# Transposing half of the activations by DMA instead of TensorE, with the contraction re-cut into chunks of 128 rows

## The chip, the cores and the metric

One core of a Trainium2 chip. The metric is the device time of one execution in microseconds (us), lower is better; medians of several executions are given. Times of the same kernel differ a little from chip to chip, so a kernel is compared only with runs of the kernel before on the same chip.

Names used below: PE is TensorE's matmul stream, PEld its weight loads, DVE is VectorE, ACT is ScalarE, POOL is GpSimd, SP is SyncE, which here only issues DMAs.

## The reference

The input `x` has 2048 tokens of 448 features. Two branches start from it and are mixed by a gate for each token.

```python
g = sigmoid((x * gate_w).sum(-1, keepdims=True))
a = A_ref(x, wq, wk, wv, wo, beta)      # q,k,v = x @ wq, x @ wk, x @ wv; 16 heads of 28; 4 segments of 512
                                        # causal softmax inside a segment + linear memory of earlier segments
b = B_ref(x, w1, b1, w2, b2)            # h = layernorm(x); u = gelu(h^T w1 + b1); y = u w2 + b2 (MLP over tokens)
return g * a + (1 - g) * b              # ... all else cut
```

For this change, two things matter. The projections `x @ wk` and so on need `x` with features on the partitions, that is, transposed. The MLP over tokens needs `x` as it is, but normalized.

## The kernel before

The kernel is a list of operations (`op`), each with an engine, an estimated cost, a priority and the buffers that it reads and writes. A planner walks through an estimated clock and gives each free engine its ready operation of best priority. What comes out is one fixed order of instructions for each engine. The chip runs that order: in the traces, the matmuls behind a waiting matmul wait with it (in e7 below, no matmul starts for 0.63 us while one waits). The kernel lets TensorE write its results to banks of PSUM, and uses a bank again when another engine has copied it out (an eviction).

```python
CK = 112                                   # contraction rows of a chunk; 4 * 112 = 448
...
load_x("SP", 0, 2)                         # tokens 0..255
op("SP", ... dma_start(wk_nat[0:CK], WK.rearrange("(c p) d -> p c d", p=CK)) ...)
load_x("SP", 2, 2)
op("ACT", ... dma_start(wvx[0:CK, :, D : D + 1], GW.rearrange("(c p o) -> p c o", p=CK, o=1) ...)   # gate_w
op("SP", ... wq, then wv, then x of tokens 512.. in blocks of 512 ...)
...
def transposes(tc):                        # token chunk tc: 512 tokens
    for half in range(2):
        ...                                # 8 PE transposes into one PSUM bank
                last = e.matmul(tb[0:CK, at : at + 128], xh[:, 4 * tc + ti, c * CK : c * CK + CK], ident[:, :],
                                is_transpose=True, start=True, stop=True, skip_group_check=True)
        ...                                # then the eviction to xT, by DVE or ACT as the planner likes
            op("DVE", lambda e, io=io: e.tensor_copy(*io()), **buse(b), reads=[bres(b)], writes=[R_xT[tc][half]],
               name=f"xTcp{tc}_{half}", cost=dve_cost(1024, 2), prio=P_PROJ + tc - 150,
               alt=("ACT", lambda e, io=io: e.activation(*io(), ACT.Copy), act_cost(1024)))

def proj_d(w_pad, R_w, hg, tc, b, t0=0, n=512):   # a projection: four matmuls over the four chunks
        for c in range(NCT):
            last = e.matmul(bank(b)[:, 0:n], w_pad[0:CK, c, hg * 128 : hg * 128 + 128],
                            xT[0:CK, c, tc * 512 + t0 : tc * 512 + t0 + n], start=(c == 0), stop=(c == NCT - 1), ...)
...
PRJ = (P_PROJ, P_PROJ + 1, P_M1 + 8.5, P_M2 + 4.5)   # chunk 2 is projected only after the MLP's unit 8
...
transposes(0); ...
for tc in (1, 2, 3):
    transposes(tc)
for t in range(NT):
    ln_stats(t)                            # DVE: statistics of the layer norm, 16 tiles
ln_coef()                                  # POOL: 1/sqrt(var), a power of 2.9 us
for t in range(NT):
    ln_apply(t)                            # DVE; the MLP's matmuls read the result
```

The order in time is: load, chunk 0 transposed and projected, chunks 1 to 3 transposed, layer norm, and then attention, MLP and the remaining projections woven together.

## Time and profile before

| | before |
|---|---|
| median time (3 runs) | 189.0 us (188.65 to 189.43) |
| span of the profiled execution | 186.4 us |
| PE busy in the span | 180.6 us, 97% |
| first projection starts | 7.80 us |
| last matmul starts | 183.64 us |
| PE transposes | 64, of which 32 for chunks 2 and 3 |

The head of the page of the kernel before gives the span and the busy time of each engine, with its share of the span and its number of instructions:

```profile
span 186.4 us, 3493 instructions
PE 180.6 (97%) x1373; PEld 87.3 (47%) x1384; DVE 154.0 (83%) x319; ACT 133.5 (72%) x171; POOL 69.6 (37%) x93
```

PE is the engine to shorten. A listed matmul time is a latency, though. Matmuls overlap, and what one costs PE is the distance from its start to the next start. The view of PE in time order of the kernel before has the columns start, length from the first start to the last end, line and operation, number of matmuls, and the idle time ahead of them:

```profile
15.45 1.50 PE L558 MATMUL t<-t 128*112 128x128 bf16 x24
...
30.57 0.29 PE L783 MATMUL t<-t 28*128 28x256 bf16 x4 [0.32 <-ACT t L792]
30.79 1.71 PE L646 MATMUL t<-t 112*128 112x449 bf16 x8
32.34 1.02 PE L589 MATMUL t<-t 112*128 112x512 bf16 x4
...
33.63 0.73 PE L820 MATMUL t<-t 128*32 128x512 bf16 x16
34.29 1.83 PE L889 MATMUL t<-t 128*128 128x448 bf16 x8
```

Line 558 is the PE transpose: 24 of them take 1.35 us from first start to what follows (the chain of waits gives that figure), 56 ns each. Line 889 is the MLP: its first matmul starts at 34.29 us. Projections of chunk 1 (lines 646 and 589) fill PE until the layer norm is ready, almost without a gap.

The waits of PE in the kernel before (line that waited, what it waited for, total us, times, longest us) confirm how few gaps there are:

```profile
PE t L528 <- DVE t L486: 1.2, 1, 1.2
PE t L589 <- ACT t L574: 0.4, 1, 0.4
PE t L783 <- ACT t L792: 0.3, 1, 0.3
```

The first is the warm-up ahead of all work. The others are 0.7 us in all (two lines of 0.3 us are left out).

At the head of the kernel PE waits for data. The chain of waits of the kernel before, cut to its first 8 us (start, us, what):

```profile
1.31 4.82 DMA t<-in_A_wk_dram
...
6.16 0.63 DVE t L536
6.79 0.34 DVE t L571
...
7.15 0.61 ACT t L574
...
7.80 0.28 PE t L589
```

The load of wk lands at 6.13 us. Then come the padding of wk (L536), two evictions (L571, L574) and the first projection (L589). The busy time of each engine in stretches of 2 us of the kernel before (the stretch and its length, then busy us and number of instructions of each engine, the clock granted to PE, the share of the DMA engines, GB/s):

```profile
core 0: us, PE busy (x) PEld busy (x) DVE busy (x) ACT busy (x) POOL busy (x), PEclk, DMA share, GB/s
...
2.00:4.00 2.00, 2.00 (x6) 0.76 (x5) 0.00 (x0) 0.54 (x1) 2.00 (x2) 1.00 0.48 111
4.00:6.00 2.00, 2.00 (x13) 1.06 (x12) 1.18 (x3) 0.00 (x0) 1.86 (x4) 1.00 1.05 340
```

From 2 to 4 us only 111 GB/s arrive, and from 4 to 6 us 340.

The layer norm's coefficients run on POOL. In time order, POOL in the kernel before:

```profile
26.93 0.21 POOL L741 TENSOR_SCALAR t<-t 128x16 f32<-128x16 f32 x1 [21.07 <-DVE t L734]
27.22 2.92 POOL L742 TENSOR_TENSOR t<-t 128x16 f32<-128x16 f32 x1
```

They can't start before DVE has the last statistics, at 26.9 us.

### The profile page before, as it was taken

How to read it: one execution, taken by the hardware profiler on the slowest of the kernel's cores; microseconds unless marked ns; L12 is line 12 of the kernel's file. 1: busy time of each engine (PE TensorE's matmuls, PEld its weight loads, DVE VectorE, ACT ScalarE, POOL GpSimd, SP SyncE). 2: the span in 40 equal slices, each digit the busy share in tenths (PEclk: the TensorE clock that was granted, in tenths of full speed). 3: DMA queues.
4: the chain of work that ended last, by engine and by line, in shares of the span. 5: the costliest groups of instructions: out<-in, count | busy, mean ns of one | idle time of the engine just before them, and what ended most of it. 6: DMA issues, size and time to landing. Idle time of an engine off the chain costs nothing.

```text
span 186.4 us, 3493 instructions
## 1 busy us (share of the span) xinstructions
PE 180.6 (97%) x1373; PEld 87.3 (47%) x1384; DVE 154.0 (83%) x319; ACT 133.5 (72%) x171; POOL 69.6 (37%) x93
## 2 busy tenths in 40 slices
PE   7999999999999999999999999999999999999994
PEld 2658434344454444434454443454454444454554
DVE  1979898998689989798998999998999987765232
ACT  2288779968999999999988979840399857620230
POOL 8200029343242534543725635171135365160200
PEclk9999999999999999999999999999999999999999
DMA  3999991001971746001341506238810072744011
GB/s 92 321 328 265 294 150 28 5 0 40 250 220 31 204 116 159 4 4 28 96 133 37 160 4 183 45 102 225 240 35 0 4 213 70 212 146 127 0 53 49
DMA packets 42596, 21.77 MB, mean 117 GB/s; under 512 B 8148, under 2 KB 42580, under 8 KB 42580
## 3 DMA queue, kind: packets, MB, share of 16 engines
q1 hardware_dynamic: 42116, 21.54, 43.7%
q8 instruction: 11, 0.18, 0.4%
q10 hardware_dynamic: 464, 0.00, 0.1%
q14 instruction: 5, 0.04, 0.1%
HBM read 18.13 MB, written 1.84 MB: 107 GB/s over the span
## 4 chain that ended last, share of the span: by engine, by line
PE 82%; DVE 6%; ACT 6%; DMA 3%; issue 1%; SPq 0%
PE t L889 24%; PE t L917 24%; PE t L589 9%; PE t L783 7%; PE t L869 6%; PE t L820 6%; PE t L646 3%; ACT t L792 3%; DMA t<-in_A_wk_dram 3%; DVE t L732 2%; PE t L670 1%; ACT t L631 1%; PE t L558 1%; DVE t L581 1%; DVE t L624 1%
## 5 line engine op out<-in xcount | busy, mean ns | idle before, releaser
L792 ACT ACTIVATE t<-t 128x2048 bf16<-128x2048 f32 (+1 forms) x48 | 76.9, 1601 | 12.5 <-PE t L783 12.2
L796 POOL TENSOR_SCALAR_AFFINE_SELECT t<-t 128x512 bf16<-128x512 bf16 x64 | 47.0, 737 | 64.2 <-ACT t L792 59.9
L889 PE MATMUL t<-t 128*128 128x448 bf16 x224 | 47.3, 353 | 0.4 <-issue 0.3
L917 PE MATMUL t<-t 128*128 128x448 bf16 (+1 forms) x238 | 46.0, 342 | 0.3
L917 PEld LDWEIGHTS t<-t 128*128 128x128 bf16 x238 | 22.2, 98 | 19.4 <-issue 1.7
L589 PE MATMUL t<-t 112*128 112x512 bf16 (+1 forms) x144 | 30.0, 356 | 0.4 <-ACT t L574 0.4
L889 PEld LDWEIGHTS t<-t 128*128 128x128 bf16 x224 | 20.2, 98 | 20.4 <-issue 2.6
L849 POOL TENSOR_TENSOR t<-t 128x448 bf16<-128x448 f32 x12 | 14.3, 1196 | 18.2 <-DVE t L847 18.2
L589 PEld LDWEIGHTS t<-t 112*128 112x128 bf16 x144 | 13.4, 98 | 13.1 <-issue 0.9
L922 DVE SCALAR_TENSOR_TENSOR t<-t 128x448 bf16<-128x448 f32 (+1 forms) x17 | 11.1, 653 | 10.0 <-PE t L917 7.5
L783 PE MATMUL t<-t 28*128 28x512 bf16 (+3 forms) x256 | 17.3, 302 | 0.8 <-ACT t L792 0.3
L875 ACT ACTIVATE t<-t 128x448 bf16<-128x448 f32 x9 | 6.6, 730 | 12.4 <-PE t L869 12.2
L646 PE MATMUL t<-t 112*128 112x449 bf16 x64 | 14.1, 354 | 0.1
L869 PE MATMUL t<-t 128*128 128x448 bf16 x64 | 13.6, 353 | 0.0
L835 DVE STREAM_TRANSPOSE t<-t 128x512 f32<-128x512 f32 x16 | 11.3, 703 | 2.6 <-PE t L820 2.6
L626 ACT ACTIVATE t<-t 128x512 bf16<-128x512 f32 x8 | 4.8, 595 | 11.4 <-PE t L589 11.4
L783 PEld LDWEIGHTS t<-t 28*128 28x128 bf16 x256 | 5.1, 91 | 16.3 <-ACT t L792 10.8
L855 DVE STREAM_TRANSPOSE t<-t 128x512 bf16<-128x512 bf16 x16 | 11.2, 698 | 1.6 <-POOL t L849 1.6
L732 DVE BATCH_NORM_STATS2 t<-t 128x6 f32<-128x448 bf16 x16 | 9.4, 611 | 3.5 <-DMA t<-in_A_x_dram 3.3
L820 PE MATMUL t<-t 128*32 128x512 bf16 (+3 forms) x256 | 11.6, 302 | 0.0
L906 DVE SCALAR_TENSOR_TENSOR t<-t 128x448 bf16<-128x448 f32 x14 | 9.2, 658 | 2.9 <-ACT t L904 2.8
L901 DVE SCALAR_TENSOR_TENSOR t<-t 128x448 f32<-128x448 f32 x14 | 9.7, 697 | 1.7 <-ACT t L896 1.7
(83 smaller groups left out, 216.1 us busy)
## 6 DMA issues: line engine op xcount, KB each, us to landing
t<-in_B_w_dram SPq DMA_DIRECT2D x7, 1024.0 KB, 6.0
t<-in_B_w_dram SPq DMA_DIRECT2D x8, 896.0 KB, 5.2
out_dram<-t SPq DMA_DIRECT2D x15, 112.0 KB, 3.0
t<-in_A_x_dram SPq DMA_DIRECT2D x3, 448.0 KB, 7.7
t<-in_A_x_dram SPq DMA_DIRECT2D x2, 224.0 KB, 4.4
t<-in_A_wk_dram SPq DMA_DIRECT2D x1, 392.0 KB, 4.8
t<-in_A_wq_dram SPq DMA_DIRECT2D x1, 392.0 KB, 5.8
t<-in_A_wv_dram SPq DMA_DIRECT2D x1, 392.0 KB, 6.6
```

The costliest lines, as they stand in the source:

```text
L589: last = e.matmul(bank(b)[:, 0:n], w_pad[0:CK, c, hg * 128 : hg * 128 + 128], xT[0:CK, c, tc * 512 + t0 : tc * 512 + t0 + n], start=(c == ...
L646: last = e.matmul(bank(b)[:, 0 : D + 1], xT[0:CK, c, t * 128 : t * 128 + 128], wvx[0:CK, c, :], start=(c == 0), stop=(c == NCT - 1), skip_ ...
L732: op("DVE", lambda e: e.bn_stats(st6[:, t, :], xh[:, t, :]), reads=[R_x[t]], writes=[R_st6[t]], name=f"bns{t}", cost=512, prio=P_PROJ - 10)
L783: last = e.matmul(bank(hl)[:, c0 : c0 + w_], kT[r, hg, s * 512 + j * 128 : s * 512 + j * 128 + 128], qT[r, hg, s * 512 + 128 * j : s * 512 ...
L792: op("ACT", lambda e: e.activation(pv, ps[:, 0:4, 0:w], ACT.Exp, scale=SCALE), reads=R_bank[0:4], writes=[R_P[u % 2][f]], name=f"exp{n}", ...
L796: op("POOL", lambda e, d=d: e.affine_select(d, d, pattern=[[0, 4], [1, 128]], compare_op=ALU.is_ge, fill=0.0, base=0, channel_multiplier=- ...
L820: last = e.matmul(bank(cb)[32 * hl : 32 * hl + 32, 128 * j : 512], vaug[:, 4 * s + j, 32 * h : 32 * h + 32], pv[:, hl, c0 : c0 + w_], star ...
L835: dv(lambda e: e.transpose(t2[:, 0, :], bank(cb)[:, 0:512]), [bres(cb)], [R_tt[tb][0]], "ta", 630, use=(cb,))
L849: op("POOL", lambda e: e.tensor_tensor(o3, n3[0], n3[1], op=ALU.add), reads=R_tt[tb], writes=[R_ob[tb]], name=f"o{u}", cost=1280, port=Tru ...
L869: last = e.matmul(bank(b)[:, 0:D], oT[:, hg, T * 128 : T * 128 + 128], wo_sb[:, hg, :], start=(hg == 0), stop=(hg == NHG - 1), skip_group_ ...
L889: op("PE", lambda e, st=st: e.matmul(bank(b)[:, 0:D], w1c[:, st, f2 * 128 : f2 * 128 + 128], xh[:, st, :], start=(st == 0), stop=(st == NT ...
L917: op("PE", lambda e, ft=ft: e.matmul(bank(b)[:, 0 : c1 - c0], w2c[:, ft, t2_ * 128 : t2_ * 128 + 128], uT[:, ft, c0:c1], start=(ft == 0), ...
```

## The change

The intent: chunks 2 and 3 of `x` are needed in transposed form only from 74.8 us on. So 32 of the 64 PE transposes can be replaced by transposes that the DMA engines make straight from DRAM, and PE, DVE and ACT get their time back. The builder accepts a DMA transpose only if its columns are a multiple of 128. (A kernel that kept the 112-row chunks did not build. The Trainium skill, "DMA: Bandwidth & Descriptors", DMA Transpose (X-bar), Constraints, says that for DRAM inputs with fewer than 128 columns software can fall back to a rearranged access pattern; this builder refused instead.) So the contraction is cut into 128-row chunks that start at rows 0, 128, 256 and 320. The fourth repeats 64 rows of the third, and the weights of these 64 rows are set to zero. For this, each weight matrix is loaded in two parts, the second from ACT's queue, and so the tiny load of `gate_w` moves from first to last on ACT's queue.

```diff
-CK = 112
+CK = 128
+C0 = (0, 128, 256, 320)
...
+    def load_w(dst, src, r, name):
+        op("SP", lambda e: e.dma_start(dst[:, 0:3, 0:D], src[0:384].rearrange("(c p) d -> p c d", p=128)), ...)
+        op("ACT", lambda e: e.dma_start(dst[64:128, 3, 0:D], src[384:448]), ...)
+
+    def transpose_x(tc):
+        for k, (c, n) in enumerate(((0, 3), (3, 1))):
+            op("SP", lambda e, c=c, n=n: e.dma_start_transpose(
+                xT[:, c : c + n, tc * 512 : tc * 512 + 512], x2[tc * 512 : tc * 512 + 512, C0[c] : C0[c] + 128 * n]),
+               writes=[R_xT[tc][k]], name=f"dtx{tc}_{k}", dma=True, cost=1200 * n, nbytes=180000 * n)
...
     load_x("SP", 0, 2)
-    op("SP", lambda e: e.dma_start(wk_nat[0:CK], WK.rearrange("(c p) d -> p c d", p=CK)), ...)
+    load_w(wk_nat, WK, R_P[0], "wk")
     load_x("SP", 2, 2)
-    op("ACT", lambda e: e.dma_start(wvx[0:CK, :, D : D + 1], GW.rearrange("(c p o) -> p c o", p=CK, o=1), ...
+    load_w(wq_nat, WQ, R_P[1], "wq")
+    load_w(wvx, WV, R_wv, "wv")
+    op("ACT", lambda e: e.dma_start(wvx[:, 0:3, D : D + 1], GW[0:384].rearrange("(c p o) -> p c o", p=128, o=1), ...
+    op("ACT", ... wvx[64:128, 3, D : D + 1], GW[384:448] ...)
+    for w, r, name in ((wk_nat, R_wz[0], "k"), (wq_nat, R_wz[1], "q"), (wvx, R_wz[2], "v")):
+        op("DVE", lambda e, w=w: e.memset(w[0:64, 3, :], 0.0), writes=[r], name="wz" + name, cost=200, prio=50.0)
...
-    for tc in (1, 2, 3):
-        transposes(tc)
+    transposes_1()                    # chunks 0 and 1 stay on PE, in 128-row form
...
     for _ in range(3):
         ring_load()                   # the first three blocks of w1
+    transpose_x(2)
+    transpose_x(3)
```

More of the change, by code (lines that the diff above doesn't have):

```diff
@@ L358, in build_kernel @@
     wqk = sb([128, 2, NCT, 512])
-    wvx = sb([128, NCT, D + 1])
+    wvx = sb([128, NCT, D + 4])
     wo_sb = sb([128, NHG, D])
@@ L409, in build_kernel @@
     R_wkp, R_wqp = R("wkp"), R("wqp")
-    R_wv, R_gw, R_wo = R("wv"), R("gw"), R("wo", 4)
+    R_wv, R_gw, R_wo, R_wz = R("wv", 2), R("gw", 2), R("wo", 4), R("wz", 3)
     R_qT = [R(f"qT{g}_", 4) for g in range(NHG)]
@@ L436, in load_x @@
            writes=R_x[t0 : t0 + n], name=f"ldx{t0}", dma=True, cost=500 if n == 2 else 1300, nbytes=n * 128 * 896)
+    def load_w(dst, src, r, name):
+        op("SP", lambda e: e.dma_start(dst[:, 0:3, 0:D], src[0:384].rearrange("(c p) d -> p c d", p=128)),
+           writes=[r[0]], name="ld" + name, dma=True, cost=500, nbytes=344064)
+        op("ACT", lambda e: e.dma_start(dst[64:128, 3, 0:D], src[384:448]), writes=[r[1]], name="ld" + name + "b",
+           dma=True, cost=500, nbytes=57344)
@@ L438, in build_kernel @@
+    def transpose_x(tc):
[3 more added lines that the diff above has]
+               writes=[R_xT[tc][k]], name=f"dtx{tc}_{k}", dma=True, cost=1200 * n, nbytes=180000 * n)
     load_x("SP", 0, 2)
-    op("SP", lambda e: e.dma_start(wk_nat[0:CK], WK.rearrange("(c p) d -> p c d", p=CK)), writes=R_P[0],
-       name="ldwk", dma=True, cost=500, nbytes=401408)
+    load_w(wk_nat, WK, R_P[0], "wk")
@@ L441, in build_kernel @@
     load_x("SP", 2, 2)
-    op("ACT", lambda e: e.dma_start(wvx[0:CK, :, D : D + 1], GW.rearrange("(c p o) -> p c o", p=CK, o=1),
+    load_w(wq_nat, WQ, R_P[1], "wq")
+    load_w(wvx, WV, R_wv, "wv")
+    op("ACT", lambda e: e.dma_start(wvx[:, 0:3, D : D + 1],
+                                     GW[0:384].rearrange("(c p o) -> p c o", p=128, o=1),
                                      allow_slow_non_contiguous=True),
-       writes=[R_gw], name="ldgw", dma=True, cost=500, nbytes=8000)
-    op("SP", lambda e: e.dma_start(wq_nat[0:CK], WQ.rearrange("(c p) d -> p c d", p=CK)), writes=R_P[1],
-       name="ldwq", dma=True, cost=500, nbytes=401408)
@@ L447, in build_kernel @@
-    op("SP", lambda e: e.dma_start(wvx[0:CK, :, 0:D], WV.rearrange("(c p) d -> p c d", p=CK)), writes=[R_wv],
-       name="ldwv", dma=True, cost=500, nbytes=401408)
-    for t0 in (4, 8, 12):
-        load_x("SP", t0, 4)
+       writes=[R_gw[0]], name="ldgw", dma=True, cost=500, nbytes=8000)
+    op("ACT", lambda e: e.dma_start(wvx[64:128, 3, D : D + 1], GW[384:448].rearrange("(p o) -> p o", o=1),
+                                     allow_slow_non_contiguous=True),
+       writes=[R_gw[1]], name="ldgwb", dma=True, cost=500, nbytes=2000)
@@ L451, in build_kernel @@
+    for w, r, name in ((wk_nat, R_wz[0], "k"), (wq_nat, R_wz[1], "q"), (wvx, R_wz[2], "v")):
+        op("DVE", lambda e, w=w: e.memset(w[0:64, 3, :], 0.0), writes=[r], name="wz" + name, cost=200, prio=50.0)
+    load_x("SP", 4, 4)
+    load_x("SP", 8, 4)
+    load_x("SP", 12, 4)
     op("SP", lambda e: e.dma_start(betab[:, :], BETA.partition_broadcast(128)), writes=[R_beta],
@@ L470, in ring_load @@
                                            w1v[:, :, k * 256 : k * 256 + 256]),
-               reads=[R_wv, R_gw], writes=[R_slot[r]], name=f"ldw1_{k}", dma=True, cost=500,
+               reads=R_wv, writes=[R_slot[r]], name=f"ldw1_{k}", dma=True, cost=500,
                nbytes=1048576)
@@ L511, in load_wo @@
                                                   WO.rearrange("(g l d) m -> l d g m", g=NHG, l=4)[hl]),
-               reads=[R_wv], writes=[R_wo[hl]], name=f"ldwo{hl}", dma=True, cost=500, nbytes=100352)
+               reads=[R_wv[0]], writes=[R_wo[hl]], name=f"ldwo{hl}", dma=True, cost=500, nbytes=100352)
     rr = [0]
@@ L537, in build_kernel @@
                                       wk_nat.rearrange("p c (h j) -> p (c h) j", j=DH)[0:CK]),
-       reads=R_P[0], writes=[R_wkp], name="padk", cost=560, port=True, prio=P_BASE)
+       reads=R_P[0] + [R_wz[0]], writes=[R_wkp], name="padk", cost=560, port=True, prio=P_BASE)
     def pad_q():
@@ L542, in pad_q, with transposes_0, fn, io @@
                                           wq_nat.rearrange("p c (h j) -> p (c h) j", j=DH)[0:CK]),
-           reads=R_P[1], writes=[R_wqp], name="padq", cost=560, port=True, prio=P_BASE)
-    def transposes(tc):
+           reads=R_P[1] + [R_wz[1]], writes=[R_wqp], name="padq", cost=560, port=True, prio=P_BASE)
+    def transposes_0(half):
+        b = next_bank()
+        def fn(e):
+            tb = bank(b).bitcast(BF16)
+            last = None
+            for c in range(4):
+                for k in range(2):
+                    last = e.matmul(tb[:, c * 256 + k * 128 : c * 256 + k * 128 + 128],
+                                    xh[:, 2 * half + k, C0[c] : C0[c] + 128], ident[:, :], is_transpose=True,
+                                    start=True, stop=True, skip_group_check=True)
+            return last
+        op("PE", fn, reads=R_x[2 * half : 2 * half + 2] + [R_ident], writes=[bres(b)], **btake(b), name=f"trx0_{half}",
+           mode="f", cost=8 * 56, prio=P_PROJ + 0.02 * half)
+        for k in range(2):
+            def io(k=k):
+                return (xT[:, 2 * k : 2 * k + 2, half * 256 : half * 256 + 256],
+                        bank(b).bitcast(BF16)[:, k * 512 : k * 512 + 512].rearrange("p (c t) -> p c t", c=2))
+            if k == 0 or half == 1:
+                op("DVE", lambda e, io=io: e.tensor_copy(*io()), reads=[bres(b)], writes=[R_xT0[half][k]],
+                   name=f"xTcp0_{half}{k}", cost=dve_cost(512, 2), prio=P_PROJ - 150)
+            else:
+                op("ACT", lambda e, io=io: e.activation(*io(), ACT.Copy), reads=[bres(b)], writes=[R_xT0[half][k]],
+                   name=f"xTcp0_{half}{k}", cost=act_cost(512), prio=P_PROJ - 150)
@@ L547, in transposes, with transposes_1, fn @@
+    def transposes_1():
         for half in range(2):
             b = next_bank()
-            parts = [(ti, c) for ti in range(4) for c in (2 * half, 2 * half + 1)]
-            if tc == 0:
-                parts = [(ti, c) for c in range(4) for ti in (2 * half, 2 * half + 1)]
-            def fn(e, b=b, parts=parts):
+            def fn(e, half=half, b=b):
                 tb = bank(b).bitcast(BF16)
                 last = None
-                for ti, c in parts:
-                    at = (c * 256 + ti % 2 * 128) if tc == 0 else (c % 2 * 512 + ti * 128)
-                    last = e.matmul(tb[0:CK, at : at + 128], xh[:, 4 * tc + ti, c * CK : c * CK + CK], ident[:, :],
-                                    is_transpose=True, start=True, stop=True, skip_group_check=True)
-                return last
@@ L562, in transposes @@
-            op("PE", fn, reads=[R_x[4 * tc + ti] for ti, c in parts] + [R_ident], writes=[bres(b)], **btake(b),
-               name=f"trx{tc}_{half}", mode="f", cost=8 * 56, prio=P_PROJ + (0.02 if tc == 0 and half else 0))
-            if tc == 0:
-                for k, on_dve in ((0, True), (1, half == 1)):
-                    def io(b=b, half=half, k=k):
-                        return (xT[0:CK, 2 * k : 2 * k + 2, half * 256 : half * 256 + 256],
-                                bank(b).bitcast(BF16)[0:CK, k * 512 : k * 512 + 512].rearrange("p (c t) -> p c t", c=2))
-                    if on_dve:
-                        op("DVE", lambda e, io=io: e.tensor_copy(*io()), reads=[bres(b)], writes=[R_xT0[half][k]],
-                           name=f"xTcp0_{half}{k}", cost=dve_cost(512, 2), prio=P_PROJ - 150)
-                    else:
-                        op("ACT", lambda e, io=io: e.activation(*io(), ACT.Copy), reads=[bres(b)],
-                           writes=[R_xT0[half][k]], name=f"xTcp0_{half}{k}", cost=act_cost(512), prio=P_PROJ - 150)
-            else:
-                def io(half=half, b=b):
-                    return (xT[0:CK, 2 * half : 2 * half + 2, tc * 512 : tc * 512 + 512],
-                            bank(b).bitcast(BF16)[0:CK, :].rearrange("p (c t) -> p c t", c=2))
-                op("DVE", lambda e, io=io: e.tensor_copy(*io()), **buse(b), reads=[bres(b)], writes=[R_xT[tc][half]],
-                   name=f"xTcp{tc}_{half}", cost=dve_cost(1024, 2), prio=P_PROJ + tc - 150,
-                   alt=("ACT", lambda e, io=io: e.activation(*io(), ACT.Copy), act_cost(1024)))
@@ new lines, in fn, with io @@
+                for ti in range(4):
+                    for c2 in range(2):
+                        c = C0[2 * half + c2]
+                        last = e.matmul(tb[:, c2 * 512 + ti * 128 : c2 * 512 + ti * 128 + 128],
+                                        xh[:, 4 + ti, c : c + 128], ident[:, :], is_transpose=True, start=True,
+                                        stop=True, skip_group_check=True)
+                return last
+            def io(half=half, b=b):
+                return (xT[:, 2 * half : 2 * half + 2, 512:1024],
+                        bank(b).bitcast(BF16).rearrange("p (c t) -> p c t", c=2))
@@ L585, in proj_d @@
+            op("PE", fn, reads=R_x[4:8] + [R_ident], writes=[bres(b)], **btake(b), name=f"trx1_{half}", mode="f",
+               cost=8 * 56, prio=P_PROJ)
+            op("DVE", lambda e, io=io: e.tensor_copy(*io()), **buse(b), reads=[bres(b)], writes=[R_xT[1][half]],
+               name=f"xTcp1_{half}", cost=dve_cost(1024, 2), prio=P_PROJ - 149,
+               alt=("ACT", lambda e, io=io: e.activation(*io(), ACT.Copy), act_cost(1024)))
     def proj_d(w_pad, R_w, hg, tc, b, t0=0, n=512):
@@ L645, in fn @@
             for c in range(NCT):
-                last = e.matmul(bank(b)[:, 0 : D + 1], xT[0:CK, c, t * 128 : t * 128 + 128], wvx[0:CK, c, :],
+                last = e.matmul(bank(b)[:, 0 : D + 1], xT[0:CK, c, t * 128 : t * 128 + 128], wvx[0:CK, c, 0 : D + 1],
                                 start=(c == 0), stop=(c == NCT - 1), skip_group_check=True)
             return last
-        op("PE", fn, reads=R_xT[t // 4] + [R_wv, R_gw], writes=[bres(b)], **btake(b), name=f"prt{t}", mode="f",
+        op("PE", fn, reads=R_xT[t // 4] + R_wv + R_gw + [R_wz[2]], writes=[bres(b)], **btake(b), name=f"prt{t}", mode="f",
            cost=pe_cost(449, 449, 449, 449), prio=PRJ[t // 4])
@@ L931, in mm2_last @@
         mm2(T, D // 2, D)
-    transposes(0)
+    transposes_0(0)
+    transposes_0(1)
     for t0 in (0, 256):
```

## The prediction

> **What bounds the kernel.** TensorE. The page's table of engines has PE busy 180.6 of 186.4 us; the waits give PE 2.5 us of idle in all. Busy could flatter, so I compared start-to-start times in PE's timeline with columns at full clock: 448-column matmuls come every 0.19 us, 512-column ones every 0.215, and the granted clock is 1.0. From the first projection (7.8 us) on, PE has almost no slack. Before it the load of wk limits: the chain of waits runs DMA (landing at 6.13), pad copy on DVE, two evictions, first projection.
>
> **Removed.** 32 PE transposes (chunks 2 and 3). In the chain 24 take 1.35 us and 8 take 0.45, 56 ns each (their listed 219 ns is latency): 1.8 us of PE. Also four evictions of 1024 columns, 0.69 us each on DVE, 1.02 on ACT; probably two on each: 1.4 us of DVE, 2.0 of ACT. All sit at 15 to 19 us.
>
> **Unchanged on PE.** Still four matmuls per projection output. 128 contraction rows in place of 112 cost and save nothing: weight loads of 112 and 128 rows both have a mean of 98 ns, matmuls of 449 and 448 columns 354 and 353. The Trainium skill says so of weight loads ("TensorE: Matmul & The Clock Gate", Step-by-step: time goes with columns, not rows); this trace agrees.
>
> **Added.** (a) Three memsets on DVE, about 0.27 us each (estimate from the warm-up memsets), in idle time before 4.8 us. (b) Five small loads from ACT's queue instead of one, 0.43 us of issue each, before ACT's first real work at 7.15 us: hidden. About 115 KB of wq and wv go ahead of wk: at the 340 GB/s of 4 to 6 us up to 0.3 us later, but two queues also fill the ramp at 2 to 4 us. I count +0.1 (-0.2 to +0.4) us on the path. (c) Four transposes on SP's queue, in sum eight times the 128 KB of a key-feature transpose. Those issue in 1.2 us and land in 2.6: some 10 us of SP and 1 MB of traffic, at 9 to 30 us, beside the first three ring loads. Results are needed only at 74.8 us (chunk 2's projections). The first ring block landed near 23.4 us and is needed at 34.3: a delay of 3 to 5 us fits. Key transposes wait longer on SP; their consumer starts at 55 us.
>
> **On the path.** The 1.8 us counts in full only if PE finds other work earlier. The first MLP matmul (34.3 us) waits for the layer norm, whose statistics end DVE's busy stretch at 26.8 us (2.9 us on POOL follow). DVE loses 1.4 us of copies just there, so it should come 1 to 1.5 us earlier; projections of chunk 2 can fill the rest.
>
> **Prediction: 187.2 us**, 80% range 186.1 to 188.7. Faster by over 2%: 5%; within 2%: 92%; slower by over 2%: 3%.
>
> **What would show it.** PE transposes 64 -> 32, same counts in all other PE groups. First projection at 7.6 to 8.2 us. First MLP matmul at 32 to 33.5 us. The x transposes landed before 40 us. PE's idle total still under 4 us.
>
> **What would make it wrong.** The x transposes are slow from DRAM, or fill SP's queue ahead of the ring loads, so that the first MLP matmul or an in-order ACT waits (a key-feature buffer is freed by a transpose): some us lost, seen as PE idle at 28 to 40 us. The layer norm does not come earlier and PE stalls before the MLP: gain near zero. wk lands later: up to 0.5 us lost. All engines' static order is planned anew from estimated costs, so switches between tiled and full matmuls can shift by some 0.5 us either way.

## The result, and the profile after

| | before | after |
|---|---|---|
| median time, 6 runs each | 189.28 us (188.65 to 189.69) | 187.47 us (187.31 to 187.63) |
| ratio, 95% interval | | 0.9906 (0.9887 to 0.9925) |
| span of the profiled execution | 186.4 us | 185.6 us |
| first projection starts | 7.80 us | 7.36 us |
| last matmul starts | 183.64 us | 182.77 us |
| between the two ("stream") | 175.84 us | 175.41 us |
| first MLP matmul starts | 34.29 us | 30.98 us |

A ratio is the mean time of one kernel's runs over that of the other's in the same rounds, so it is not quite the ratio of the medians quoted. The verdict is "the same within 2%": a gain of about 1%. On another chip the same two kernels gave 188.49 and 187.55 us, a ratio of 0.9944. The kernel before varies from chip to chip (medians of 189.28, 188.95, 188.49 and 188.96), and the kernel after hardly does (187.47 and 187.55). The traces show about 0.9 us between the kernels: 0.88 us of span before rounding, 0.87 us at the last matmul. The traced execution of before took 188.43 us, less than any of its six timed ones; that of after took 187.34 us. So about half of the measured 1.8 us is not in these two traces, and I leave that half open. What follows explains the 0.9 us.

The time of 187.47 us lies within 0.3 us of the prediction. But the table already shows that it was not earned as predicted: 1.8 us of PE work was removed, but the stream from first to last matmul became only 0.43 us shorter, and as much again came from the head, where a small loss had been expected.

The head of the page of the kernel after, the lines that answer to those of before:

```profile
span 185.6 us, 3441 instructions
PE 179.6 (97%) x1352; PEld 84.9 (46%) x1352; DVE 153.3 (83%) x321; ACT 132.0 (71%) x168; POOL 72.2 (39%) x93
```

The chain of waits of the kernel after, first 8 us:

```profile
0.79 2.99 DMA t<-in_A_x_dram
...
3.80 1.15 DVE t L761 x2
...
5.10 1.24 DVE t L553
6.35 0.34 DVE t L583
...
6.71 0.61 ACT t L586
...
7.36 0.72 PE t L618 x5
```

Both loads at the head land about 1 us earlier: the first block of x at 3.78 us (4.79 before), wk at 5.03 us (6.13 before). In both kernels DVE does two statistics of x before the padding of wk (L553); here they end just after wk has landed, and so the chain names x. The padding starts at 5.10 us, 1.06 us earlier than before, and takes 0.6 us longer. What remains is 0.44 us. The padding ends at 6.32 to 6.35 us in all nine traces with the new loads, although it starts anywhere from 5.06 to 5.37 us, and in each of them the memsets that POOL does at the head end at 5.84 to 5.87 us. That POOL's memsets slow the padding, and so cap what the earlier loads bring, fits these times; no run moved them. The same stretches of 2 us, kernel after:

```profile
2.00:4.00 2.00, 2.00 (x6) 0.76 (x5) 0.37 (x2) 0.15 (x1) 2.00 (x2) 1.00 0.93 286
4.00:6.00 2.00, 2.00 (x15) 0.99 (x13) 2.00 (x5) 1.13 (x1) 1.87 (x4) 1.00 1.00 279
```

From 2 to 4 us, 286 GB/s arrive in place of 111.

PE in time order, kernel after, the same stretches as before:

```profile
16.55 1.04 PE L618 MATMUL t<-t 128*128 128x512 bf16 x4 [0.40 <-DVE t L633]
...
29.88 0.40 PE L812 MATMUL t<-t 28*128 28x512 bf16 x4 [0.32 <-ACT t L689]
...
30.98 0.35 PE L918 MATMUL t<-t 128*128 128x448 bf16 x1
31.59 1.85 PE L918 MATMUL t<-t 128*128 128x448 bf16 x7 [0.26 <-DVE t L777]
33.85 0.73 PE L849 MATMUL t<-t 128*32 128x512 bf16 x16 [0.41 <-ACT t L689]
```

The MLP (line 918) indeed starts 3.3 us earlier. But look at the pace: these eight matmuls take 2.3 us of PE from start to start, where 8 times 0.19 us would be 1.5 us. They wait for the layer norm's products (line 777): DVE takes about 0.33 us for each, and does two evictions of 0.6 us in between. POOL in time order, kernel after, shows that the first operation of the layer norm's coefficients came 2.24 us earlier, and the power 1.83 us earlier:

```profile
24.69 0.62 POOL L770 TENSOR_SCALAR t<-t 128x16 f32<-128x16 f32 x1 [18.83 <-DVE t L783]
25.39 2.92 POOL L771 TENSOR_TENSOR t<-t 128x16 f32<-128x16 f32 x1
```

And the waits of PE in the kernel after:

```profile
PE t L545 <- DVE t L503: 1.2, 1, 1.2
PE t L618 <- ACT t L586: 0.6, 1, 0.6
PE t L849 <- ACT t L689: 0.4, 1, 0.4
PE t L618 <- DVE t L633: 0.4, 1, 0.4
PE t L812 <- ACT t L689: 0.3, 1, 0.3
PE t L918 <- DVE t L777: 0.3, 1, 0.3
PE t L835 <- DVE t L717: 0.2, 1, 0.2
```

The first two lie before or at the first projection. The other five are waits in the stream, 1.6 us, against 0.3 us in the second trace of before (after its own first projection only L783 waits for any length there).

The DMA transposes themselves, line 447 of the kernel after, with their time on SP's queue (minimum, median, maximum in ns) and their time to landing:

```profile
L447 SPq DMA_TRANSPOSE t<-in_A_x_dram x4: 1262/2740/4444, 10.1 to 29.2; - x4
...
DMA to landing us min/median/max: 3.0/5.1/7.7
```

The last one starts at 29.2 us and takes at most 7.7 us, so all have landed before 37 us. Nothing needs them before 73.49 us, when chunk 2's projections start. Nobody waits for them.

### How the stream is accounted for

In what follows, "stream" is the time from the start of the first projection to the start of the last matmul, read from the records of PE. It leaves out the head and the tail. "PE work" of some matmuls is their number times the start-to-start distance that the trace shows where nothing waits (0.19 us at 448 columns, 0.215 at 512, 0.056 for a transpose of 128).

### The profile page after: what moved, and what is told of

Read it like the earlier page. It is cut to its first block, busy times and chain, and to the rows that moved or that the text cites. A ratio compares the mean times of both kernels' runs of the same rounds, so it can differ in the third digit from the quotient of the medians.

```text
span 185.6 us, 3441 instructions
## 1 busy us (share of the span) xinstructions
PE 179.6 (97%) x1352; PEld 84.9 (46%) x1352; DVE 153.3 (83%) x321; ACT 132.0 (71%) x168; POOL 72.2 (39%) x93
## 3 DMA queue, kind: packets, MB, share of 16 engines
HBM read 18.13 MB, written 1.84 MB: 108 GB/s over the span
## 4 chain that ended last, share of the span: by engine, by line
PE 80%; DVE 8%; ACT 5%; POOL 3%; DMA 2%; issue 1%
PE t L946 24%; PE t L918 23%; PE t L618 11%; PE t L812 7%; PE t L849 5%; PE t L898 5%; PE t L675 4%; DVE t L761 2%; ACT t L821 2%; DMA t<-in_A_x_dram 2%; POOL t L771 2%; PE t L835 2%; PE t L699 1%; ACT t L612 1%; ACT t L686 1%
## 5 line engine op out<-in xcount | busy, mean ns | idle before, releaser
L825 POOL TENSOR_SCALAR_AFFINE_SELECT t<-t 128x512 bf16<-128x512 bf16 x64 | 48.0, 751 | 66.8 <-ACT t L821 59.3
L618 PE MATMUL t<-t 128*128 128x512 bf16 (+1 forms) x144 | 30.4, 356 | 1.0 <-ACT t L586 0.6
L946 PEld LDWEIGHTS t<-t 128*128 128x128 bf16 x238 | 22.2, 98 | 19.4 <-issue 1.7
L918 PEld LDWEIGHTS t<-t 128*128 128x128 bf16 x224 | 20.1, 98 | 21.0 <-issue 2.6
L618 PEld LDWEIGHTS t<-t 128*128 128x128 bf16 x144 | 13.2, 98 | 14.0 <-issue 1.1
L878 POOL TENSOR_TENSOR t<-t 128x448 bf16<-128x448 f32 x12 | 15.5, 1293 | 9.7 <-DVE t L876 9.7
L904 ACT ACTIVATE t<-t 128x448 bf16<-128x448 f32 x10 | 7.2, 724 | 12.7 <-PE t L898 12.7
L675 PE MATMUL t<-t 128*128 128x449 bf16 x64 | 14.1, 354 | 0.0
L935 DVE SCALAR_TENSOR_TENSOR t<-t 128x448 bf16<-128x448 f32 x14 | 10.0, 719 | 2.2 <-ACT t L933 2.1
L930 DVE SCALAR_TENSOR_TENSOR t<-t 128x448 f32<-128x448 f32 x14 | 8.4, 608 | 1.6 <-ACT t L925 1.6
L849 PEld LDWEIGHTS t<-t 128*32 128x32 bf16 x256 | 5.4, 96 | 8.7 <-issue 5.3
```

Source lines behind the costliest of these rows:

```text
L675: last = e.matmul(bank(b)[:, 0 : D + 1], xT[0:CK, c, t * 128 : t * 128 + 128], wvx[0:CK, c, 0 : D + 1], start=(c == 0), stop=(c == NCT - 1 ...
L825: op("POOL", lambda e, d=d: e.affine_select(d, d, pattern=[[0, 4], [1, 128]], compare_op=ALU.is_ge, fill=0.0, base=0, channel_multiplier=- ...
L849: last = e.matmul(bank(cb)[32 * hl : 32 * hl + 32, 128 * j : 512], vaug[:, 4 * s + j, 32 * h : 32 * h + 32], pv[:, hl, c0 : c0 + w_], star ...
L878: op("POOL", lambda e: e.tensor_tensor(o3, n3[0], n3[1], op=ALU.add), reads=R_tt[tb], writes=[R_ob[tb]], name=f"o{u}", cost=1280, port=Tru ...
L918: op("PE", lambda e, st=st: e.matmul(bank(b)[:, 0:D], w1c[:, st, f2 * 128 : f2 * 128 + 128], xh[:, st, :], start=(st == 0), stop=(st == NT ...
L946: op("PE", lambda e, ft=ft: e.matmul(bank(b)[:, 0 : c1 - c0], w2c[:, ft, t2_ * 128 : t2_ * 128 + 128], uT[:, ft, c0:c1], start=(ft == 0), ...
```

## The experiments

Five explanations compete. The expectations, written before each run, use single letters as running labels: A is "PE counts", B "Copies count", C "Head" or "Order", D "Only both" in the list here. The letters of e8, e9 and e11 are explained in their own expectations.

- **PE counts**: the removed PE transposes are the gain, nearly all of it.
- **Copies count**: the four removed evictions on DVE and ACT are the gain, by way of an earlier layer norm.
- **Only both**: PE, DVE and ACT pass work to each other in a fixed order, so each alone gives little when removed.
- **Head**: the re-cut weight loads, not the transposes, bring the gain.
- **Order**: the plan of all engines was made anew, and some of the difference is an accident of the new order.

To tell the order from the work, e1 to e3 and e5 to e7 pin the order. The edit is put inside an operation whose cost and dependencies the planner still sees as they were, so every other instruction stays where it was.

### e0: the kernel before once more

No edit. It gives the noise, and a second trace.

> Control: the kernel before, unchanged, timed against itself. Every theory expects a ratio of 1.000 within about 0.003. Its profile says what varies from run to run: if the first x load lands at 3.8 us here (it took until 4.8 in the profile of before, 3.8 in that of after), the 0.44 us earlier start of the projections in after is chance; if it lands at 4.8 again, the new loads may have to do with it. I expect it to vary.

Measured: 189.0 us, ratio to before 0.9997 (0.9985 to 1.001); stream 175.83 us, against 175.84 us in the first trace. Streams of the same kernel agree to some hundredths of a microsecond (the kernel after: 175.41, and 175.43 in e4). The start of the first projection varies more, from 7.80 to 7.99 us. Differences of a tenth in the stream can therefore be read.

### e1, e2, e3: put the removed work back into the kernel after

**e1** runs 32 more PE transposes ahead of chunk 1's second half, with no copies.

```diff
             def fn(e, half=half, b=b):
                 tb = bank(b).bitcast(BF16)
+                for x in range(32 if half else 0):
+                    e.matmul(tb[:, x % 8 * 128 : x % 8 * 128 + 128], xh[:, 4 + x % 4, 0:128], ident[:, :],
+                             is_transpose=True, start=True, stop=True, skip_group_check=True)
```

> The kernel after with 32 more PE transposes of 128x128 (results overwritten), just before those of chunk 1, and not one other instruction moved: only PE's time is put back. Theory A (PE's time is what was saved, and PE is full): 1.4 to 1.8 us slower than after, so 188.9 to 189.3. Theory B (the lightened DVE and ACT are what counted, through the layer norm): under 0.5 us slower. Theory C (loads at the head, or the newly planned order): under 0.5 us slower. A middle value, 0.7 to 1.2, would say that after has waits near 16 and 30 us that swallow part of PE's work.

**e2** leaves PE alone and puts copies back: two of 1024 columns on ACT (1.04 us each), two of 496 fp32 columns on DVE (0.67 us each).

```diff
+            def twice(e, half=half, io=io, b=b):
+                e.activation(spare[:, half, :], bank(b).bitcast(BF16), ACT.Copy)
+                return e.activation(*io(), ACT.Copy)
...
-               alt=("ACT", lambda e, io=io: e.activation(*io(), ACT.Copy), act_cost(1024)))
+               alt=("ACT", twice, act_cost(1024)))
...
+        def b1c_and_two(e):
+            for i in (2, 3):
+                e.tensor_copy(spare[:, i, 0:496], ps[:, b, 16:512])
+            return e.tensor_copy(b1c[:, :], bps[:, 0:NFT])
```

> The kernel after with four evictions put back at 14 to 17 us (two on ACT of 1024 columns, two on DVE of 496 fp32 columns, into a spare place), PE untouched, no other instruction moved. Theory A: 0 to 0.4 us slower than after. Theory B: 1.0 to 1.5 us slower, as the layer norm comes that much later and the first MLP matmul with it. Theory C: about 0.

**e3** is both edits together.

> The kernel after with the 32 PE transposes and the four evictions put back together. Theory A: as with the transposes alone or little more, 1.5 to 2.0 us slower than after, which is the time of before. Theory B: 1.0 to 2.0 us slower, nearly all of it there with the evictions alone. Theory C: clearly faster than before still (under 0.8 us slower than after).

Measured, all on one chip, where before had 188.95 us (the kernel after was not run there, so its stream is from its own traces):

| | median us | ratio to before (95%) | stream us | stream, less after's 175.42 |
|---|---|---|---|---|
| e1, PE work back | 189.25 | 1.001 (0.9997 to 1.0022) | 177.05 | +1.63 |
| e2, copies back | 189.56 | 1.0025 (1.0013 to 1.0038) | 177.26 | +1.84 |
| e3, both back | 190.22 | 1.0071 (1.0057 to 1.0085) | 178.19 | +2.77 |

Two things follow. First, the size of the PE work was right. The chain of waits of e1 (start, us, what) shows 1.79 us for the 32 added transposes:

```profile
15.43 1.79 PE t L597 x32
```

Added to the kernel after, they cost nearly all of that, 1.63 us. Second, the copies alone cost as much, although PE has nothing more to do in e2. (The dose is not quite the right one. The trace of before has three of its six 1024-column evictions on DVE, 0.69 us each, and three on ACT, 1.02 us each; the kernel after has two left, both on ACT. So 2.1 us of DVE and 1.0 us of ACT were removed, and e2 puts 1.3 and 2.1 us back. That such copies reach PE is shown; that the removed ones were worth 1.8 us is not.) They come back as waits of PE, as the waits of PE in e2 show (line 622 is the projection, line 637 the DVE eviction that it waits for):

```profile
PE t L622 <- DVE t L637: 1.5, 2, 1.1
```

In the kernel after, PE waits 0.4 us for that eviction. From start to start, e2 loses 1.31 us at 26.5 us and 0.45 us at 17.5 us that after does not lose there. e3 costs less than e1 and e2 summed (2.77 against 3.47 us), so the two partly hide each other. Finally, e3 does about the work of the kernel before in the order of after, and is slower than before by 0.7%: taken with all that work, the new order is no better than the old.

### e4 to e7: take the work out of the kernel before

**e4** is the kernel after on the chip of this group.

> Control: the kernel after, unchanged, beside the kernel before on this chip, so that the runs of this call and the last can be compared. Every theory: ratio 0.9906 within 0.003. In the trace: first projection at 7.3 to 7.7 us (7.36 once; 7.63, 7.67 and 7.34 in the three kernels with the same loads, 7.80 and 7.99 in two traces of before).

**e5** leaves out 28 of the 32 PE transposes of chunks 2 and 3 (the copies read the one block that is left; the result is wrong). **e6** keeps the transposes and cuts the four copies to 64 columns. **e7** is both.

```diff
-                for ti, c in parts:
+                for ti, c in parts[: 1 if tc > 1 else 8]:          # e5, e7
```
```diff
                 def io(half=half, b=b):
+                    if tc > 1:                                      # e6
+                        return (xT[0:CK, 2 * half : 2 * half + 2, tc * 512 : tc * 512 + 32],
+                                bank(b).bitcast(BF16)[0:CK, :].rearrange("p (c t) -> p c t", c=2)[:, :, 0:32])
```

(This is e6's form; e7 reads the same number of columns from the one block that is left.)

e6 fills the rest of xT with zeros beforehand, and still passed the comparison with the reference. So passing is no evidence that an edit there is harmless.

> The kernel before with 28 of the 32 PE transposes of chunks 2 and 3 taken out and no other instruction moved; the four evictions read the one remaining transposed block four times over (so the result is wrong on purpose), with the same size. No DMA transpose, no 128-row contraction, loads as before. Theory A (PE's time is what counts): 1.6 us faster than before, ratio 0.9917. Theory D (at 14 to 30 us PE, DVE and ACT hand work to one another in a fixed order, so that the transposes and the evictions each hold up the rest, and taking out one leaves the other): 0.2 to 1.0 us faster. Theory B (evictions alone count): under 0.2 us.

> The kernel before with all PE transposes, and the four evictions of chunks 2 and 3 cut from 1024 to 64 columns (two memsets at the head, in DVE's idle time, fill the rest; the result is wrong on purpose); no other instruction moved. Theory A: 0 to 0.2 us faster. Theory B: 1.5 us faster or more. Theory D: 0.2 to 1.0 us faster.

> The kernel before with both cuts, no instruction moved, nothing put in their place (wrong on purpose). Theory A: 1.6 us faster, as with the PE cut alone. Theory B: as with the copies cut alone. Theory D: 1.6 to 2.2 us, more than the sum of the two single cuts. If it is well under 1.6, PE waits for something else in this order, and what the change got beyond it came from the new order or the loads.

Measured on one chip, where before had 188.49 us:

| | median us | ratio to before (95%) | stream us | stream, less before's 175.84 |
|---|---|---|---|---|
| e4, after | 187.55 | 0.9944 (0.9932 to 0.9956) | 175.43 | -0.41 |
| e5, PE work out | 188.12 | 0.9977 (0.9965 to 0.9989) | 175.46 | -0.38 |
| e6, copies out | 188.53 | 0.9997 (0.9986 to 1.0009) | 175.84 | 0.00 |
| e7, both out | 187.58 | 0.9954 (0.9942 to 0.9967) | 174.85 | -0.99 |

e5 takes 1.57 us of PE work away (28 times 0.056 us), and the stream gets 0.38 us shorter. PE only gets sooner to places where it waits for DVE or ACT: 0.57 us in the middle of the transposes, 0.19 and 0.25 us at two projections that wait for an eviction, and 0.16 us more than before at the wait for ACT near 30 us. These sum to what is missing. e6 takes copies away and gains nothing, since PE comes no sooner. Together, in e7, the stream gets 0.99 us shorter; 0.57 us is again lost in the middle of the transposes. PE in time order in e7:

```profile
16.37 0.26 PE L563 MATMUL t<-t 128*112 128x128 bf16 x1
17.00 0.26 PE L563 MATMUL t<-t 128*112 128x128 bf16 x1 [0.36 <-DVE t L722]
17.10 2.11 PE L597 MATMUL t<-t 112*128 112x256 bf16 x11
```

The view names line 722, a memset of one column outside PSUM. What ended 8 ns before it is an eviction of chunk 1, as DVE in time order in e7 shows:

```profile
15.62 0.59 DVE L740 BATCH_NORM_STATS2 t<-t 128x6 f32<-128x448 bf16 x1
16.25 0.69 DVE L589 COPY t<-t 112x1024 bf16<-112x1024 bf16 x1
```

Of the DVE operations that end just then, it is the only one that can have freed a PSUM bank, and DVE did a statistic of the layer norm ahead of it. This is the theory of "only both". It also shows how much of a perfect removal of work the fixed order lets through: 0.38 of 1.57 us for PE alone, 0.99 us with the copies as well.

One more number from the traces places these losses. Take the start of the power on POOL (2.92 us, the layer norm's coefficients), counted from the first projection. In each of the six runs with a pinned order it moves by what the stream moves, to within 0.02 us: +1.62 in e1, +1.84 in e2, +2.78 in e3, -0.38 in e5, 0.00 in e6, -1.00 in e7. So everything that these runs gain or lose is settled before the layer norm. From before to after it moves by 1.38 us, and the stream by 0.43 only. By this measure 0.4 of the 1.79 us removed was lost ahead of the layer norm, and about 1.0 us behind it, in waits of the new order.

### e8: the new loads and the 128-row layout, all transposes on PE

The kernel after, but chunks 2 and 3 are transposed on PE as chunk 1 is. No DMA transposes of x. The plan is made anew.

```diff
-    transposes_1()
+    for tc in (1, 2, 3):
+        transposes_1(tc)               # as transposes_1 of the kernel after, with the token chunk as argument
...
-    transpose_x(2)
-    transpose_x(3)
```

> Half of the change: loads and 128-row contraction with its overlapping fourth chunk as in after, but x of chunks 2 and 3 transposed by PE and evicted as in before (order planned anew). The first projection starts at 7.34 to 7.67 us in five traces with these loads and at 7.80 to 7.99 in five with the old ones. Theory H (the new loads bring some 0.35 us at the head, contraction over 128 rows costs and brings nothing): 0.2 to 0.5 us faster than before, ratio about 0.998, projections' matmuls at the same mean times. Theory L (the loads are noise, all the gain is the transposes): ratio 1.000 within 0.001. Theory K (the layout itself brings most of the gain): ratio under 0.996.

Measured: 187.39 us, where before had 188.96 us on the same chip; ratio 0.9924 (0.9912 to 0.9936). The kernel that removes nothing from PE gains as much as the kernel with DMA transposes (e9, next, on the same chip: 0.9926). Its stream is 175.22 us, 0.62 us under before's, and its first projection starts at 7.34 us. It has all 64 PE transposes, and the mean times of the projection matmuls are as before, so neither fewer transposes nor the 128 rows as such explain the 0.62 us. What is left, by exclusion and not by a run of its own, is the order: the trace shows fewer waits in the stream. The waits of PE in e8, from 0.2 us up, all of them:

```profile
PE t L545 <- DVE t L503: 1.2, 1, 1.2
PE t L918 <- DVE t L777: 0.2, 1, 0.2
PE t L946 <- issue: 0.2, 1, 0.2
```

The 0.3 us wait for ACT at 30.6 us in the kernel before is absent. The rest of the 0.62 us I could not trace to single waits.

### e9: the DMA transposes of x later on SP's queue

The kernel after, with the four DMA transposes behind the first loads of w1 instead of the first of them ahead.

```diff
-               writes=[R_xT[tc][k]], name=f"dtx{tc}_{k}", dma=True, cost=1200 * n, nbytes=180000 * n)
+               writes=[R_xT[tc][k]], name=f"dtx{tc}_{k}", dma=True, cost=1200 * n, nbytes=180000 * n, rel=20000.0)
```

> After, with the four x transposes planned no earlier than 20 us, so that SP issues them behind the first three ring loads and not one ahead of them (at 10 us). Theory S (where they stand in SP's queue does not matter, their results are wanted at 75 us and the first ring block early enough): the time of after within 0.3 us, PE's waits the same. Rival: the early one holds up the loads of wo and of the ring by 3 to 4 us, and this costs something: 0.3 us or more faster than after.

Measured: 187.62 us, ratio 0.9926 (0.9914 to 0.9939), stream 175.09 us. Where the transposes stand on SP is worth a few tenths at most, and no wait of PE in either kernel is for a load of w1. Their place in the SP queue is not what ate the gain. e9 still has their traffic, so it doesn't test that, but none of PE's waits in the stream of either kernel is for a DMA.

### e10: chunk 1 by DMA too

If removing 16 more PE transposes and two copies paid as the first 32 were meant to, this would be faster again.

```diff
     load_x("SP", 4, 4)
+    transpose_x(1)
     load_x("SP", 8, 4)
...
-    transposes_1()
```

> The change carried on: chunk 1 transposed by DMA too, issued between the loads of x for chunks 1 and 2; 16 fewer PE transposes (0.9 us) and two fewer evictions on ACT (2 us). By my theory A of the prediction, 0.9 us faster than after. Theory D (in this stretch a saving is turned into waits for the other engines, about half of it stayed when both were cut in before): 0.3 to 0.6 us faster. But chunk 1 is wanted at 15 us: if its DMA lands later than that, or holds up the loads of the later x (on which the statistics and the layer norm wait), PE waits by 16 to 32 us and it is no faster, or slower.

Measured: 189.45 us (188.77 to 190.7), ratio 1.0032 (1.0008 to 1.0055), so slower than before; stream 177.62 us. The two DMA transposes hold SP from 4.01 to 11.15 us, and the loads of the later x stand behind them. PE in time order in e10:

```profile
30.18 0.29 PE L813 MATMUL t<-t 28*128 28x256 bf16 x4 [1.62 <-ACT t L822]
31.78 0.40 PE L813 MATMUL t<-t 28*128 28x512 bf16 x4 [1.32 <-ACT t L690]
32.58 3.14 PE L919 MATMUL t<-t 128*128 128x448 bf16 x8 [0.40 <-DVE t L778]
```

PE has run out of projections, and waits 1.62 and 1.32 us for ACT. Then the profile shows a granted clock of 0.5 for 3.41 us, and MLP matmuls come 0.37 us apart in place of 0.19. So this idle time had a second price. It isn't what undid e10, though: one of the six runs shows a mean clock of 1.0, and it took 188.77 us, still 1.2 us more than e9; four runs at 0.991 took 189.18 to 189.62 us, one at 0.981 took 190.7 us.

### e11: make the planner expect a later layer norm

The waits at 31 us in the kernel after begin because the planner starts the MLP as soon as the first layer-norm product is due. If the planner were told a longer time for the power on POOL, it would put other matmuls first. This tests whether the 0.8 us lost at the slow start of the MLP can be had for nothing.

```diff
-            op("POOL", fn, reads=reads, writes=writes, name=name, cost=2900 if name == "rstd" else 200, prio=P_BASE)
+            op("POOL", fn, reads=reads, writes=writes, name=name, cost=4400 if name == "rstd" else 200, prio=P_BASE)
```

> After, with only one planning number altered: the layer norm's power on POOL is told to the planner as 4.4 us in place of 2.9 (it takes 2.9 us, but its successors wait for other POOL work, so that the normalised x comes 5 us after the statistics). The engines' static order then puts the evictions of v and the next key features ahead of the first layer-norm product on DVE. Theory W (after loses about 1 us to waits that come of its static order near 30 to 34 us, where DVE stands still for POOL and ACT and PE for DVE): 0.4 to 0.9 us faster than after, with PE's waits at 30 to 34 us gone. Rival: the order there makes no difference, or is lost again later: within 0.3 us of after.

Measured: 188.08 us, ratio 0.9958 (0.9946 to 0.997), stream 176.07 us: 0.65 us longer than after's, not shorter. This theory failed. The new order brought new waits of 0.89 us at 30.8 us, 0.56 us at 61.5 us and 0.65 us at 66.1 us. The waits are not one mistake in the plan. Each order has its own.

### What the head owes to the load of gate_w

No experiment isolates this; it is read from fourteen traces. In the nine with the new loads, the first projection starts at 7.33 to 7.67 us, mean 7.44; in the five with the old, at 7.80 to 7.99 us, mean 7.90. The two groups don't overlap, and e8, which has no DMA transposes of x, belongs to the first. So the new loads, or the 128-row layout that came with them, give 0.46 us.

The trace of before suggests how. `gate_w` is 448 values for 112 partitions, so its load is 448 packets of 2 bytes, and it is the first thing on ACT's queue. They run from 1.87 to 4.24 us, while the first x and wk are to be loaded on SP's queue. From 2.5 to 3.5 us the 896-byte packets of x and wk get through at 51 and 65 per half microsecond. In the kernel after, where `gate_w` runs only from 5.85 to 9.84 us, 190 and 186 get through in the same time. The Trainium skill states a mechanism that fits ("DMA: Bandwidth & Descriptors", Queues, rings and completion order): each DMA engine takes packets from its queues in turn. It also gives 512 bytes as the least size for full rate (Specifications). The counts fit both: 254 packets of SP's queue and 406 of ACT's pass between 2 and 4 us, at a DMA share of 0.48 and 111 GB/s; after, 590 and 81, at 0.93 and 286 GB/s. The kernel after offers a second look: from 6 to 8 us, when `gate_w`'s packets run there, the rate is 189 GB/s at a share of 0.78, against 279 and 350 GB/s in the stretches on either side. What the traces don't show is why the engines lose so much: a 2-byte packet is listed with 9 ns, and at a share of 0.48 the engines stand idle for half of the time.

What stays open: the change also altered the shape of the weight loads and added 64-row loads on ACT's queue. The edit that would separate these, the kernel before with nothing but its `gate_w` load held back, was not run.

## Why the prediction was right or wrong

**Right in the number, by luck.** 187.2 us (186.1 to 188.7) was predicted, and 187.47 us measured. The predicted gain on PE came in part only, a gain at the head made up for a part of the rest, and half of the measured 1.8 us is not in the traces at all; on another chip the two kernels were 0.94 us apart.

**Right: the size of the removed PE work.** The prediction's 1.8 us of PE, 56 ns for each of 32 transposes, was 1.79 us in e1.

**Wrong: the step "the 1.8 us counts in full only if PE finds other work earlier [...] projections of chunk 2 can fill the rest".** This was the main term, and the stream became only 0.43 us shorter. The projections of chunk 2 did not fill anything. They start at 73.49 us (74.79 before), because the plan ranks them behind the MLP's unit 8, and I had that ranking before me. What stands between 15 and 34 us is work that DVE and ACT have to hand over first. The waits that stand in the stream of after can be named, counted from start to start: 0.40 us ahead of 16.55 us for a DVE eviction, 0.32 us ahead of 29.88 us for ACT, 0.77 us from 30.98 us on for layer-norm products that come one by one, 0.41 us ahead of 33.85 us for ACT, and 0.37 us at 69.4 us for a DVE operation. That is 2.3 us. The same count gives 0.7 us in the second trace of before. The balance asks for 1.4 us more (1.79 less 0.43), and these give 1.6 us; the small rest I did not trace. The wait at 16.55 us lies ahead of the layer norm, where 0.4 us was lost; the others lie behind its coefficients and belong to the new order. e5 and e7 show losses of the first kind with the order of before: 0.38 and 0.99 us gained of 1.57. No run took the second kind away; e11 tried, and got other waits.

**Wrong in sign: the head, "+0.1 (-0.2 to +0.4) us".** It was about -0.45 us, and the first projection at 7.36 us lies outside my 7.6 to 8.2 (the second trace of after, in e4, has 7.61). I counted the bytes that go ahead of wk, and took the slow 2 to 4 us of before for a ramp. The bytes were the wrong quantity. The 448 smallest packets on the other queue are the likely cost (no run isolates them), and the change happens to move them out of the way. I had listed this load in the diff and its queue in the page, 464 packets with no bytes to speak of.

**About right for the layer norm, too little for the MLP: "it should come 1 to 1.5 us earlier".** The first of its coefficients' operations started 2.24 us earlier (26.93 to 24.69 us), the power that follows 1.83 us earlier (27.22 to 25.39 us), of which 0.45 us is the head's: 1.38 us remain. But the first MLP matmul came 3.3 us earlier, at 30.98 us and outside my 32 to 33.5. I had guessed two of the removed evictions on each engine; three were DVE's, 2.1 us. That the copies alone moved the layer norm is not so: put back, they delay the power to 27.55 us (e2), but the PE work alone delays it to 27.29 us (e1), and in e6, without them but in the old order, the first MLP matmul stays at 34.39 us. In any case, the earlier start of the MLP was no gain in itself, since its next matmuls then waited.

**Right: the 128 rows cost and save nothing.** Means of projection matmuls and weight loads are the same in before, after and e8. **Right: SP and the DMA traffic are no obstacle.** All transposes of x had landed before 37 us (40 predicted), PE's waits sum to 3.4 us (under 4 predicted), and e9 shows that their place matters little.

**Right as a caution: "can shift by some 0.5 us either way".** A new plan gave -0.6 us in e8 and +0.65 us in e11. This is as large as the effect under study, and it is why the edits that keep the order fixed were needed.

**Summed up.** About half of what the traces show as gained, 0.44 of 0.87 us, comes from the head, and the DMA transposes take no part in it. The other half, 0.43 us, is the 1.8 us of PE work less the waits. It can't be credited to the DMA transposes with certainty either, since the order changed with them and e8 gets as far without moving one transpose. No run beat both kernels clearly: e8 and after are equal within what the chips differ by.

## What to carry to other kernels

Here, work removed from the busiest engine paid only up to the next place where that engine waits for another in a fixed order. Put the same work back, or take it out, with the order pinned, and read what the waits make of it before counting it as gain. And look at the number of packets in the first microseconds, not only at the bytes: here a load of 448 elements of 2 bytes at the head of a second queue went with 111 GB/s in place of 286 for the loads that everything waits for.

## What the Trainium skill lacked or had wrong

- "DMA: Bandwidth & Descriptors": it has turn-taking by packet and the 512-byte limit in different sections, but not what follows for two queues. Here, while 448 packets of 2 bytes ran on one queue for 2.4 us, both together moved 111 GB/s, against 286 GB/s without them (two kernels compared; no run isolates it). It could say that a load of single elements belongs behind the loads that something waits for.
- "Advanced Engine Details and Errata", X-Bar Transpose (TRN2): it calls transposing DMAs as fast as regular ones. The runs show what it leaves out, the time on the issuing queue: the first transpose of 384 KB held SP's queue for 3.09 us, the shortest hold by any transpose of x was 1.26 us (128 KB), and a plain load of 336 KB at the head held it for 0.46 us. Behind other transfers plain loads held it long too (3.50 us for one of w1 in after). With two more transposes early on (e10), later loads were issued some 7 us later.
- "TensorE: Matmul & The Clock Gate", Part 4: it gives about 275 ns for a PE transpose in a kernel's context. Here the listed time is about 220 ns, and in a run of 24 each costs PE 56 ns from start to start. That is the figure to use for what a transpose costs, and the page has it only for plain matmuls.
- The same page, Part 1: an idle window of about 3.4 us is to halve the clock. e10 shows that PE need not be idle throughout: waits of 1.62, 1.32 and 0.40 us with four small matmuls between each were followed by a clock of 0.5 for 3.41 us.
